# Spreading the last 128 tokens of an attention-then-experts kernel over four wider chunks

## The chip, the core and the metric

The kernel runs on one core of a Trainium2 chip. The metric is the device time of one execution, in microseconds (us), on that core; lower is better.

## The reference

A polynomial-sketch attention feeds a mixture of four dense experts. All inputs and outputs are float32.

```python
# attention: batch 4, heads 4, sequence 1088, head_dim 32, r = 8
phi = lambda x: outer(S1 @ x, S2 @ x)              # 64 features a token
num, den = phi(q) @ (phi(k).T @ v), phi(q) @ phi(k).sum(0)
x = (num / (den + 1e-6)).reshape(4352, 128)        # tokens x (heads*head_dim)
# experts: D = 128, E = 4, F = 1024
p = domain_probs / (domain_probs.sum(-1, keepdims=True) + 1e-9)
for e in range(4):
    out += p[:, e:e+1] * (np.maximum(x @ w1[e], 0) @ w2[e])
```

Nearly all arithmetic is in the experts: every token passes four times through a 128x1024 and a 1024x128 matrix.

## The kernel before

**Chunks.** The 4352 tokens are worked off in 11 chunks (`CHUNKS`, L101): chunk 0 of 128 tokens, chunk 1 of 448, chunks 2 and 3 of 480, chunks 4 to 9 of 448, chunk 10 of 128. Each chunk has 16 steps (`NQ`), four for each expert; a step handles two blocks of 128 hidden units. A half step is one block, and the program numbers half steps from the start: 32 to a chunk, so half step 160 is the first of chunk 5. The order of all work is written out by hand in half steps: which part of the attention runs when (`FIRST_AT`, `KEYS_AT`, `UNITS_AT`, L824 to L834), and which matmul of the second layer runs how many half steps after its expert began (`DEAL`, `DEAL_MORE`, `DEAL_ALL`, L75 to L88).

**A wide chunk** (1 to 9) computes with split operands: a float32 operand is replaced by two or three parts that TensorE multiplies at the fast float32 rate. The first layer of a block is three matmuls into one PSUM buffer: L1171, L1172, then a copy in place on ScalarE (L1173), then L1223. The second layer of a block is either three split matmuls (L1295 with `ha`, `hb`, `hd`), for which ScalarE makes `ha` (L1227), VectorE `hb` (L1199) and, for two blocks at once, `hd` (L1202); or one *plain* float32 matmul (L1295 with `hid`), for which ScalarE alone makes `hid` (L1232). Which blocks are split is fixed for each chunk and expert: six (`THREE`), seven (`MORE_IN`) or eight (`ALL_IN`).

**Closing an expert.** The second layer adds up in two PSUM banks, `o0` and `o1`. ScalarE copies `o0` to `ev` (L1298; one buffer); in the last chunks it copies `o1` to `rest` (L1331) and GpSimd adds `rest` to `ev` (L1334; in earlier chunks VectorE adds `o1`, L1328). GpSimd then multiplies by the gate (L1341) and adds to the chunk's running `total` (L1343), each in two pieces. After the fourth expert VectorE transposes `total` (L1306) and SyncE stores it with four DMAs (L1309).

**Narrow chunks** (0 and 10) are computed plainly: `both` (L274) splits each matmul in halves of 64 columns (all on L272), for chunk 10 the first three steps use L1141; ReLU is on ScalarE (L1149) and VectorE (L1145) in turn; the gate is applied by VectorE (L1260, L1264), and one DMA stores the result (L1269). The first-layer and second-layer weights in float32 have been overwritten by their parts by then, so `load_last` (L988) reads them again in the middle of chunk 9. Chunk 10's tokens are the last 128 of batch 3, so the loads of batch 3's queries, of the gate's probabilities and the stores treat that batch's rows in two pieces (L128, L326, L566, L1313).

**Attention beside it.** For the last three batches, a *unit* of 512 or 576 query tokens is projected, stored to a scratch tensor and read back in two arrangements (`unit_rows`, L797 and L799, four transfers of 256 or 288 KB on SyncE's queue), multiplied on VectorE (`unit_product`, L811, two halves) and then attended (`unit_visit`). Each row of `UNITS_AT` gives, for a unit, the half steps of its transpose, of its two products and of its visit; a unit's `unit_rows` follows the visit of the unit before. So for unit 5 the transfers are issued at half step 175, and its products stand at 191 and 196.

Of the kernel before, what the change touches and what calls it, by code (L numbers as in the profile page):

```python
# [24 lines left out]
def kernel(  # L25
# [24 lines left out]
    nc = tc.nc  # L50
# [17 lines left out]
    FULL = 3  # L68
# [19 lines left out]
    )  # L88
    ALL_IN = {(7, 2), (8, 2), (9, 2)}
# [11 lines left out]
    CHUNKS = [P, 448, 480, 480] + [448] * 6 + [P]  # L101
    NC = len(CHUNKS)
    MORE_IN = {(2, 2), (3, 2), (4, 2), (5, 0), (5, 2), (5, 3), (6, 2), (7, 0), (7, 1), (7, 2), (7, 3), (8, 0), (8, 1), (8, 2), (8, 3), (9, 0), (9, 1), (9, 2), (9, 3)}
    MORE_AT = {0: (61, 62), 1: (56, 57), 2: (38, 39), 3: (77, 78)}
# [16 lines left out]
    def load_rows(src, b, name, part=slice(0, S)):  # L121

        d = kn if name == "kn" else qn
        if b not in d:
            d[b] = lpool.tile([P, S], F32, tag=name, name=name)
        c, n = part.start, part.stop - part.start
        base = src.offset + b * H * S * D
        if name == "qn" and b == B - 1:  # L128
            for c, n, t in ((0, (G - 4) * D, 0), ((G - 4) * D, 4 * D, S - P)):
                nc.sync.dma_start(d[b][:, c : c + n], bass.AP(src.tensor, base + t * D, [[S * D, H], [n, 32], [1, n]]))  # L130
        else:
            nc.sync.dma_start(d[b][:, part], bass.AP(src.tensor, base + c, [[G * D, P], [1, n]]))
# [34 lines left out]
    def load_w2(e, k, to=None):  # L167
        of = OTHER if k else THREE
        w2_of[e, k] = cpool.tile([P, len(of) * DM], F32, tag=f"w2_{e}{k}", name="w2_sb")[:, :] if to is None else to
        runs = []  # L170
        for b in of:
            if runs and b == runs[-1][1]:
                runs[-1][1] += 1
            else:
                runs.append([b, b + 1])
        for b, z in runs:
            at = split_at(b)
            nc.sync.dma_start(
                w2_of[e, k][:, DM * at : DM * (at + z - b)].rearrange("p (g d) -> p g d", d=DM),
                w2[e, P * b : P * z].rearrange("(g p) d -> p g d", p=P),  # L180
            )
# [7 lines left out]
    def three_of(m, e):  # L189
        return tuple(range(FB)) if (m, e) in ALL_IN else MORE if more(m, e) else THREE  # L190

    def deal_of(m, e):
        return DEAL_ALL if (m, e) in ALL_IN else DEAL_MORE if more(m, e) else DEAL
# [24 lines left out]
    ends = cpool.tile([P, 2, E], F32, name="ends")  # L218
    e_sum = cpool.tile([P, 2, 3], F32, name="e_sum")
# [106 lines left out]
    for p0, n, g0, m, t in ((0, 96, 0, G, 0), (96, 32, 0, G - 4, 3 * S), (96, 32, G - 4, 4, B * S - P)):  # L326
        nc.scalar.dma_start(
            _ap(dp, p0, n, g0 * E, [[1, m * E]]),
            bass.AP(domain_probs.tensor, domain_probs.offset + t * E, [[m * E, n], [1, m * E]]),
        )  # L330
    for i, t, g in ((0, 0, G), (1, B * S - P, 4)):
        nc.gpsimd.dma_start(
            ends[:, i, :], bass.AP(domain_probs.tensor, domain_probs.offset + t * E, [[g * E, 32], [1, 4 * E]])
        )
# [11 lines left out]
    def gate_sums():  # L346
        add = lambda out, in0, in1: nc.gpsimd.tensor_tensor(out=out, in0=in0, in1=in1, op=ALU.add)
        nc.gpsimd.memset(pn[:, G * E :], 0.0)
        add(e_sum[:, :, 0:2], ends[:, :, 0:2], ends[:, :, 2:4])
        add(e_sum[:, :, 2], e_sum[:, :, 0], e_sum[:, :, 1])  # L350
# [4 lines left out]
    def gate_quotients():  # L355
        nc.vector.tensor_scalar(
            out=e_sum[:, :, 2], in0=e_sum[:, :, 2], scalar1=1e-9, scalar2=1.0, op0=ALU.add, op1=ALU.mult
        )
        nc.vector.reciprocal(e_sum[:, :, 2], e_sum[:, :, 2])
        for i in range(2):  # L360
            nc.vector.tensor_scalar(
                out=ends[:, i, :], in0=ends[:, i, :], scalar1=e_sum[:, i, 2:3], scalar2=None, op0=ALU.mult
            )
# [37 lines left out]
    x_last = cpool.tile([P, P], F32, name="x_last")  # L401
    ring = cpool.tile([P, 3 * CW], F32, name="ring")
    PLACES = [(0, P, x_first, 0), (P, START[3], ring, 3 * CW - START[3] + P)]
    PLACES += [(START[m], START[m + 1], ring, (m - 3) % 3 * CW) for m in range(3, NC - 1)]
    PLACES += [(START[-1], B * S, x_last, 0)]
# [158 lines left out]
    def unit_parts(b, c, n):  # L564

        return [(0, n - P), (n - P, P)] if b == B - 1 and c + n == S else [(0, n)]  # L566

# [4 lines left out]
    def query_turns(b, c, n, qT):  # L572


        for c0, m in unit_parts(b, c, n):
            src = c + c0
            if b == c == 0:
                todo = [([[1, m]], [[1, m]], 0, 0)]
            elif c0:
                todo = [([[32, 4], [1, 32]], [[1, 4], [4, 32]], 0, 0)]  # L580
            else:
                T = blocks(m)
                if T[0] == T[1]:
                    todo = [([[32 * T[0], 4], [32, T[0]], [1, 32]], [[32, 4], [P, T[0]], [1, 32]], 0, 0)]
                else:
                    todo = [
                        ([[32 * T[s], 2], [32, T[s]], [1, 32]], [[32, 2], [P, T[s]], [1, 32]], 64 * T[0] * s, HP * s)
                        for s in range(2)
                    ]
            for i, o, ci, co in todo:  # L590
                nc.vector.transpose(_ap(qT, 0, P, c0 + co, o), _ap(qn[b], 0, P, src + ci, i))
                yield
# [66 lines left out]
    def attend_products(b, c, n, qp):  # L659

        nd = [psum(ps_h, "h") for _ in range(1 if sum(blocks(m)[0] for _, m in unit_parts(b, c, n)) < 4 else 2)]
# [3 lines left out]
        for c0, m in unit_parts(b, c, n):  # L665
# [154 lines left out]
    def add(hs, run):  # L820
# [12 lines left out]
        (172, 191, 196, 207), (200, 217, 219, 223),  # L833
# [152 lines left out]
    w_last = {}  # L986

    def load_last():  # L988

        for e, (tag, width) in enumerate((("kn", S), ("vn", H * NT * D), ("qn", S), ("vx", NT * H * (D + 1)))):  # L990
            w1_of[e] = (cpool if tag == "vx" else lpool).tile([P, width], F32, tag=tag, name="w1_last")
            nc.sync.dma_start(w1_of[e][:, 0:F], w1[e])
            if e == 0:
                w_last[0] = apool.tile([P, E - 1, N3 * DM], F32, tag="kp", name="w2_last")
                w_last[1] = cpool.tile([P, N3 * DM], F32, tag="kT", name="w2_last")
            load_w2(e, 0, w_last[0][:, e] if e < E - 1 else w_last[1][:, :])

# [101 lines left out]
    def plain(m):  # L1099
        return m in (0, NC - 1)  # L1100
# [21 lines left out]
    def first(i, work, between=None):  # L1122
# [3 lines left out]
        if plain(m):  # L1126
# [7 lines left out]
            elif i in made_hp:  # L1134
                hp = made_hp.pop(i)
            else:
                hp = psum(ps_h, "h")
                for j in range(2):
                    w = w1_of[e][:, P * (2 * f + j) : P * (2 * f + j + 1)]
                    if m and kq < FULL:  # L1140
                        nc.tensor.matmul(hp[:, n * j : n * j + n], w, x_last[:, :], start=True, stop=True)  # L1141
                    else:
                        both(hp[:, n * j : n * j + n], w, (x_last if m else x_first)[:, :], start=True, stop=True)
            if m and kq % 2:
                nc.vector.tensor_scalar(  # L1145
                    out=hd[:, 0 : 2 * n], in0=hp[:, 0 : 2 * n], scalar1=0.0, scalar2=None, op0=ALU.max
                )
            else:
                nc.scalar.activation(hd[:, 0 : 2 * n], hp[:, 0 : 2 * n], ACTF.Relu)  # L1149
# [17 lines left out]
        for j in range(2):  # L1167
            k = 2 * f + j
            g = psum(ps_h, "h")[:, 0:n]
            w = slice(P * k, P * (k + 1))  # L1170
# [63 lines left out]
    def second(i, j=None):  # L1234
# [4 lines left out]
        if plain(m):  # L1239
# [16 lines left out]
            if f == NP - 1:  # L1256
                p_e = ends[:, 1 if m else 0, e : e + 1]
# [9 lines left out]
                if e == E - 1:  # L1267
                    t, to = (B * S - P, [[DM, P], [1, DM]]) if m else (0, [[G * DM, 32], [1, 4 * DM]])
                    nc.sync.dma_start(bass.AP(out.tensor, out.offset + t * DM, to), total.pop(m)[:, :])  # L1269
# [14 lines left out]
    def passed(m, e, what, k, hd):  # L1284
# [9 lines left out]
        w, h = (second_weight(e, k), hd) if what == "x" else (w2_parts[e][k]["abd".index(what)], hd["abd".index(what)])  # L1294
        nc.tensor.matmul(acc[m, e][o][:, 0:n], w, h, start=first_one, stop=last)  # L1295
        if last and o == 0:
            evs[m, e] = mpool.tile([P, CW], F32, tag="ev", bufs=1, name="ev")
            nc.scalar.activation(evs[m, e][:, 0:n], acc[m, e][0][:, 0:n], ACTF.Copy, scale=1.0 + R12)  # L1298
        if last and o == 1:
            close(m, e)  # L1300

    def turn_back(m, src):
# [4 lines left out]
        for b, c, nn, at in parts(m):  # L1307
            for a in range(4):
# [4 lines left out]
                        [[(G - 4 if b == B - 1 else G) * DM, 32], [DM, nn // 32], [1, 32]],  # L1313
# [4 lines left out]
    def gather(m, e):  # L1318
# [27 lines left out]
        if not plain(later):  # L1346
            load_gates(later, [(e + 2) % E])
        if e == E - 1:
            yield
            yield  # L1350

            for _ in range(0 if m + 2 < NC else 4):
                yield
# [28 lines left out]
    for m in range(2, NC - 1):  # L1382
# [53 lines left out]
    for i in range(len(steps) + LA):  # L1436
        if i < len(steps):
# [13 lines left out]
            if kq == NQ - 4 and 0 < m < NC - 2:  # L1451
# [20 lines left out]
            if m == NC - 2 and kq == NQ // 2:  # L1472
                assert have[0] == B * S and not plan
                load_last()
# [5 lines left out]
        if NQ * (NC - 1) <= i < NQ * (NC - 1) + 2:  # L1480
            continue
        if not behind(2 * i + 1):
            next(ending, None)

# [28 lines left out]
```

## Time and profile before

| | |
|---|---|
| median of 3 runs | 445.8 us (445.8 to 446.19) |
| the profiled execution | 445.93 us |
| its span, first to last instruction | 444.1 us |
| TensorE busy | 438.3 us (99%) |
| VectorE / ScalarE / GpSimd busy | 382.7 / 341.9 / 166.5 us |
| TensorE's granted clock | 1.00 of full |

The span is 1.8 us shorter than the time: what lies around the instructions. "Busy" is the union of an engine's instruction times; TensorE's matmuls overlap, and a busy TensorE is one that always has a matmul in flight. In a timeline a row gives start, duration, engine, line, operation, what it writes and reads, and in brackets the idle time before it with what ended it. The pace of TensorE is read from the starts of successive matmuls, not from their durations.

### The profile page before, as it was taken

The numbers are of one execution on the slowest core, as the hardware profiler recorded it, in microseconds if no ns is written. First come the engines' busy times: TensorE is split into PE (matmuls) and PEld (weight loads), VectorE is DVE, ScalarE is ACT, GpSimd is POOL, SyncE is SP. The second block draws the span as 40 slices with busy tenths as digits, with TensorE's granted clock in tenths as the row PEclk, the third lists the DMA queues.
The fourth block names the chain that finished last, engine by engine and source line by source line (L and its number), as shares of the span: only waits on it lengthen the run. The fifth ranks groups of instructions, "written<-read, shape, count | busy, mean of one in ns | idle before, by whom it ended". The sixth has DMA issues, their size and how long they took to land.

```text
span 444.1 us, 8644 instructions
## 1 busy us (share of the span) xinstructions
PE 438.3 (99%) x2995; PEld 371.3 (84%) x2995; DVE 382.7 (86%) x624; ACT 341.9 (77%) x731; POOL 166.5 (37%) x249
## 2 busy tenths in 40 slices
PE   8999999999999999999999999999999999999996
PEld 5887678888887888888888888888889888888986
DVE  5998969978999889989997998799989898998942
ACT  4478888858877688868885888687888888988831
POOL 7348523312142023313341353133445634554560
PEclk9999999999999999999999999999999999999999
DMA  6966375224502340245024601352201120015601
GB/s 175 288 183 166 84 171 118 77 50 122 156 24 45 106 107 22 63 91 142 22 43 88 124 21 32 89 126 53 57 21 21 25 61 22 21 42 173 202 1 29
DMA packets 51156, 38.46 MB, mean 87 GB/s; under 512 B 24968, under 2 KB 45384, under 8 KB 51112
## 3 DMA queue, kind: packets, MB, share of 16 engines
q1 hardware_dynamic: 49672, 36.79, 32.8%
q0 software_dynamic: 1216, 1.06, 1.1%
q8 instruction: 23, 0.38, 0.4%
q14 instruction: 21, 0.17, 0.1%
q10 hardware_dynamic: 224, 0.07, 0.1%
HBM read 32.68 MB, written 5.21 MB: 85 GB/s over the span
## 4 chain that ended last, share of the span: by engine, by line
PE 94%; DMA 4%; DVE 1%; issue 0%; ACT 0%; POOL 0%; SPq 0%; DVEq 0%; ACTq 0%
PE o L1295 40%; PE h L1223 13%; PE h L1171 13%; PE h L1172 13%; PE h L272 7%; PE o L1277 3%; PE o L272 3%; DMA w_sb<-in_moe_w_dram 3%; PE h L467 1%; DMA dp<-in_moe_domain_probs_dram 1%; DVE hb L1199 0%; DMA s_raw<-in_S_dram 0%; PE h L1141 0%; DVE qp L811 0%; DVE words L281 0%
## 5 line engine op out<-in xcount | busy, mean ns | idle before, releaser
L1173 ACT ACTIVATE h<-h 128x448 f32<-128x448 f32 (+1 forms) x288 | 155.5, 540 | 60.3 <-PE h L1172 54.6
L1199 DVE SCALAR_TENSOR_TENSOR hb<-h,ha 128x448 fp32r<-128x448 f32 (+1 forms) x226 | 137.0, 621 | 24.5 <-ACT ha L1227 22.5
L1202 DVE SCALAR_TENSOR_TENSOR hd<-ha,hb 128x896 fp32r<-128x896 f32 (+3 forms) x121 | 135.0, 1116 | 12.4 <-PE o L1295 1.1
L1171 PE MATMUL h<-xa,wa 128*128 128x448 f32 (+1 forms) x288 | 127.0, 441 | 0.0
L1227 ACT ACTIVATE ha<-h 128x448 fp32r<-128x448 f32 (+1 forms) x226 | 124.1, 549 | 0.0
L1223 PE MATMUL h<-xd,wd 128*128 128x448 f32 (+1 forms) x288 | 106.9, 371 | 0.1
L1172 PE MATMUL h<-xb,wb 128*128 128x448 f32 (+1 forms) x288 | 106.2, 369 | 0.0
L1341 POOL TENSOR_TENSOR ev<-ev,gate 128x256 f32<-128x256 f32 (+2 forms) x54 | 46.2, 855 | 139.1 <-DVE ev L1328 131.5
L1295 PE MATMUL o<-ha,vab 128*128 128x448 f32 (+1 forms) x204 | 75.8, 371 | 0.0
L1171 PEld LDWEIGHTS h<-xa,wa 128*128 128x128 f32 x288 | 54.2, 188 | 15.7 <-issue 10.7
L1172 PEld LDWEIGHTS h<-xb,wb 128*128 128x128 f32 x288 | 54.2, 188 | 15.5 <-issue 11.1
L1295 PE MATMUL o<-hd,vd 128*128 128x448 f32 (+1 forms) x204 | 62.4, 373 | 0.0
L1223 PEld LDWEIGHTS h<-xd,wd 128*128 128x128 f32 x288 | 54.0, 187 | 7.6 <-ACT h L1173 1.4
L1343 POOL TENSOR_TENSOR total<-total,ev 128x256 f32<-128x256 f32 (+2 forms) x54 | 55.9, 1035 | 4.2
L1295 PE MATMUL o<-hb,vb 128*128 128x448 f32 (+1 forms) x136 | 50.3, 370 | 0.4 <-DVE hb L1199 0.4
L1334 POOL TENSOR_TENSOR ev<-ev,rest 128x256 f32<-128x256 f32 (+1 forms) x28 | 19.9, 731 | 69.8 <-ACT rest L1331 69.8
L1295 PE MATMUL o<-hid,w_sb 128*128 128x448 f32 (+1 forms) x92 | 43.0, 549 | 0.0
L1295 PEld LDWEIGHTS o<-hd,vd 128*128 128x128 f32 x204 | 37.8, 188 | 4.7 <-issue 0.8
L1295 PEld LDWEIGHTS o<-ha,vab 128*128 128x128 f32 x204 | 38.3, 188 | 3.8
L1232 ACT ACTIVATE hid<-h 128x448 f32<-128x448 f32 (+1 forms) x62 | 34.2, 551 | 1.0 <-PE h L1223 0.8
L1295 PEld LDWEIGHTS o<-hb,vb 128*128 128x128 f32 x136 | 25.5, 188 | 3.6 <-DVE hb L1199 1.1
L1341 POOL TENSOR_TENSOR total<-ev,gate 128x256 f32<-128x256 f32 (+2 forms) x18 | 14.9, 848 | 35.3 <-issue 19.9
(159 smaller groups left out, 500.2 us busy)
## 6 DMA issues: line engine op xcount, KB each, us to landing
gate<-gates SPq DMA_DIRECT2D x22, 224.0 KB, 3.3
kn<-in_k_dram SPq DMA_DIRECT2D x4, 544.0 KB, 6.9
vn<-in_v_dram SPq DMA_DIRECT2D x16, 128.0 KB, 4.6
qp<-qd SPq DMA_DIRECT2D x8, 256.0 KB, 3.3
w_last<-in_moe_w_dram SPq DMA_DIRECT2D x4, 512.0 KB, 5.6
qp<-qd SPq DMA_DIRECT2D x6, 288.0 KB, 4.9
qb<-qd SPq DMA_DIRECT2D x6, 288.0 KB
w_sb<-in_moe_w_dram SPq DMA_DIRECT2D x3, 512.0 KB
```

The costliest lines, as they stand in the source:

```text
L272: nc.tensor.matmul(out(s), weights(s), moving(s), **flags)
L1171: nc.tensor.matmul(g, wa[:, e, w], xa, start=True, stop=False)
L1172: nc.tensor.matmul(g, wb[:, e, w], xb, start=False, stop=True)
L1173: nc.scalar.activation(g, g, ACTF.Copy, scale=1.0 + R12)
L1199: nc.vector.scalar_tensor_tensor(out=hb, in0=g, scalar=0.0, in1=high, op0=ALU.max, op1=ALU.subtract)
L1202: nc.vector.scalar_tensor_tensor(out=d2, in0=a2.bitcast(F32), scalar=R12, in1=b2.bitcast(F32), op0=ALU.mult, op1=ALU.subtract)
L1223: nc.tensor.matmul(g, w, x, start=False, stop=True, skip_group_check=True)
L1227: nc.scalar.activation(ha, g, ACTF.Relu, scale=NEAR)
L1232: nc.scalar.activation(hid[i][j], g, ACTF.Relu)
L1295: nc.tensor.matmul(acc[m, e][o][:, 0:n], w, h, start=first_one, stop=last)
L1341: nc.gpsimd.tensor_tensor(out=to[:, x], in0=ev[:, x], in1=g[:, x], op=ALU.mult)
L1343: nc.gpsimd.tensor_tensor(out=total[m][:, x], in0=total[m][:, x], in1=ev[:, x], op=ALU.add)
```

## The change

The last chunk goes; its 128 tokens are given to chunks 4 to 7, which become 480 tokens wide. The order is now 128, 448, six chunks of 480, two of 448. What goes with it: `load_last`, the two-piece treatment of batch 3 and of the probabilities. The last expert of the last chunk (9, 3) splits six blocks instead of seven, in the order `THREE + OTHER`, so that the two plain blocks come last (`DEAL_END`); the last plain matmul is made in two halves of 224 tokens; GpSimd applies the gate to `o0` alone, VectorE to `o1`, adds, transposes and stores each half by itself (`finish`), with the DMAs alternating between SyncE's and ScalarE's queues. Two places in the hand-written order move: a split of expert 0's weights (`MORE_AT`) from steps 61, 62 to 73, 75, and unit 5's first product from half step 191 to 180.

```diff
+    DEAL_END = dict(
+        a0=4, b0=4, a1=4, b1=5, a2=5, a3=5, d0=6, d1=6, b2=6, a4=7, b3=7, a5=8, b4=8, d2=8, d3=8,
+        b5=9, d4=10, d5=10, x6=10, x7=11,
+    )
...
-    CHUNKS = [P, 448, 480, 480] + [448] * 6 + [P]
+    CHUNKS = [P, 448] + [480] * 6 + [448] * 2
...
-    MORE_AT = {0: (61, 62), 1: (56, 57), 2: (38, 39), 3: (77, 78)}
+    MORE_AT = {0: (73, 75), 1: (56, 57), 2: (38, 39), 3: (77, 78)}
...
-        (172, 191, 196, 207), (200, 217, 219, 223),
+        (172, 180, 196, 207), (200, 217, 219, 223),
...
-    for p0, n, g0, m, t in ((0, 96, 0, G, 0), (96, 32, 0, G - 4, 3 * S), (96, 32, G - 4, 4, B * S - P)):
-        nc.scalar.dma_start(
...
+    nc.scalar.dma_start(
+        _ap(dp, 0, P, 0, [[1, G * E]]), bass.AP(domain_probs.tensor, domain_probs.offset, [[G * E, P], [1, G * E]])
+    )
...
-    def load_last():
...
     def plain(m):
-        return m in (0, NC - 1)
+        return m == 0
+    def at_end(m, e):
+        return (m, e) == (NC - 1, E - 1)
...
+        for x in halves(n) if last and o and at_end(m, e) else [slice(0, n)]:
+            nc.tensor.matmul(acc[m, e][o][:, x], w, h[:, x], start=first_one, stop=last, skip_group_check=at_end(m, e))
         if last and o == 0:
             evs[m, e] = mpool.tile([P, CW], F32, tag="ev", bufs=1, name="ev")
             nc.scalar.activation(evs[m, e][:, 0:n], acc[m, e][0][:, 0:n], ACTF.Copy, scale=1.0 + R12)
+            if at_end(m, e):
+                ev, g = evs.pop((m, e)), gate[m, e]
+                for x in halves(n):
+                    nc.gpsimd.tensor_tensor(out=ev[:, x], in0=ev[:, x], in1=g[:, x], op=ALU.mult)
+                    nc.gpsimd.tensor_tensor(out=total[m][:, x], in0=total[m][:, x], in1=ev[:, x], op=ALU.add)
         if last and o == 1:
-            close(m, e)
+            finish(m, e) if at_end(m, e) else close(m, e)
+    def finish(m, e):
+        n = CHUNKS[m]
...
+        for x in halves(n):
+            nc.vector.tensor_tensor(out=rest[:, x], in0=g[:, x], in1=o1[:, x], op=ALU.mult)
+            nc.vector.tensor_tensor(out=rest[:, x], in0=rest[:, x], in1=whole_sum[:, x], op=ALU.add)
+            nc.vector.transpose(ob[:, x], rest[:, x])
+            t, r = (c + x.start) // 32, (x.stop - x.start) // 32
+            for a in range(4):
+                (nc.scalar if a % 2 else nc.sync).dma_start(
...
```

## The prediction

> **What bounds the kernel.** I read the page's busy shares first, then the chain that ended last, then the busy time by chunk, then TensorE's rows, and last what runs after the last wide matmul.
>
> ```profile
> PE 438.3 (99%) x2995; PEld 371.3 (84%) x2995; DVE 382.7 (86%) x624; ACT 341.9 (77%) x731; POOL 166.5 (37%) x249
> ...
> PE 94%; DMA 4%; DVE 1%; issue 0%; ACT 0%; POOL 0%; SPq 0%; DVEq 0%; ACTq 0%
> ```
>
> TensorE is 94% of the chain, so a matmul added in the middle is time added, and one removed is time saved, unless TensorE waits there. By chunk (4 to 8, and the end from TensorE's first narrow matmul on):
>
> ```profile
> core 0: us, PE busy (x) PEld busy (x) DVE busy (x) ACT busy (x) POOL busy (x), PEclk, DMA share, GB/s
> 173.34:216.09 42.75, 42.75 (x234) 35.98 (x233) 39.42 (x59) 33.97 (x73) 12.45 (x15) 1.00 0.33 82
> 216.09:259.98 43.89, 43.89 (x299) 38.44 (x298) 38.56 (x60) 34.32 (x73) 14.49 (x17) 1.00 0.35 70
> 259.98:304.56 44.58, 44.21 (x267) 37.21 (x266) 39.96 (x64) 33.70 (x71) 14.70 (x17) 1.00 0.28 67
> 304.56:343.90 39.34, 39.34 (x189) 35.24 (x188) 35.46 (x53) 34.72 (x75) 15.14 (x17) 1.00 0.21 43
> 343.90:383.47 39.57, 39.57 (x191) 35.42 (x189) 35.54 (x49) 34.91 (x74) 19.39 (x23) 1.00 0.14 30
> ...
> 423.10:444.10 21.00, 17.45 (x258) 16.27 (x257) 7.56 (x16) 5.01 (x12) 6.61 (x9) 1.00 0.09 16
> ```
>
> First number: length of the stretch. TensorE fills the chunks that grow (only the third has 0.37 us of idle), and VectorE, at 39.42 of 42.75, is not far behind it. The change buys the narrow chunk's time with wider matmuls in four chunks, so the forecast is a difference of two numbers near 10 us.
>
> **1. Four chunks grow by 32 tokens.** Chunks 4 to 7 hold 171, 177, 171 and 183 split matmuls, 702 in all, and 7, 5, 7 and 3 plain ones, 22. The pace is read from starts in the chain: two pieces of chunk 2 (480 tokens) and two of chunk 8 (448), in each case six matmuls apart.
>
> ```profile
> 110.29 0.65 PE o L1295 x3
> 111.60 0.65 PE o L1295 x3
> ...
> 351.13 0.61 PE o L1295 x3
> 352.35 0.61 PE o L1295 x3
> ```
>
> (111.60 - 110.29)/6 = 0.218 us against (352.35 - 351.13)/6 = 0.203; two decimals allow a difference of 0.0143 to 0.0150, and I take 0.0147: 702 x 0.0147 = 10.3 us. A piece with a plain matmul (one split, then two passes) takes 1.02 us at 480 and 0.95 at 448 in the same chain, so a plain one grows by 0.07 - 0.015 = 0.055: 22 x 0.055 = 1.2 us. **Sum +11.5.** From above 702 x 0.0150 + 1.2 = 11.7; from below, by the durations of L1223 (379 against 369 ns), 702 x 0.010 + 1.2 = 8.2, which is far off because durations overlap. Check: 183 x 0.203 + 3 x 0.75 = 39.4 for chunk 8, measured 39.57. ScalarE and VectorE grow less (L1199 from 614 to 646 ns, 5%) and stay behind TensorE's 7%.
>
> The Trainium skill ("TensorE: Matmul & The Clock Gate", Back-to-back issue gap) says that successive warm matmuls start N/2.4 + 2.5 ns apart; as an estimate 32 columns would then cost 13.3 ns, not 14.7, and the four passes of a plain one 53 ns: 10.5 us in place of 11.5.
>
> **2. The end.** TensorE's order is the same in both kernels up to the last matmul of expert (9, 2), at 418.69 us before. What follows lasts 444.1 - 418.7 = 25.4 us before, narrow chunk included.
>
> ```profile
> 418.69 0.36 PE L1295 MATMUL o<-hd,vm 128*128 128x448 f32 x1
> ...
> 425.39 0.60 POOL L1343 TENSOR_TENSOR total<-total,ev 128x192 f32<-128x192 f32 x1
> 426.46 0.55 ACT L1298 ACTIVATE ev<-o 128x448 f32<-128x448 f32 x1 [1.10 <-PE o L1295]
> ...
> 430.51 0.73 POOL L1343 TENSOR_TENSOR total<-total,ev 128x256 f32<-128x256 f32 x1
> 431.20 0.60 POOL L1341 TENSOR_TENSOR ev<-ev,gate 128x192 f32<-128x192 f32 x1
> ...
> 440.61 0.35 DVE L1264 SCALAR_TENSOR_TENSOR end<-o,ends,end 128x128 f32<-128x128 f32 x1 [0.89 <-PE o L272]
> 440.99 0.36 SPq L1269 DMA_DIRECT2D out_dram<-end  x1
> ```
>
> After, in the times of before: TensorE still has 28 split matmuls (5.7 us) and two plain blocks (0.75 each) from 418.89 on, so it is done at about 426.2. GpSimd is later. It closes expert (9, 2) at 425.99 (second row: 425.39 + 0.60), and `ev` has one buffer, so ScalarE can't copy `o0` of (9, 3) earlier: 426.04 to 426.6 (L1298, 0.55). Behind that copy on ScalarE stand only its four store DMAs. Then four GpSimd operations of 224 columns, 0.67 each (between 0.60 for 192 and 0.73 for 256), with 0.06 between: the first half of `total` at 428.1, the second at 429.45. VectorE has made the first product of gate and `o1` by 426.4 and waits: add (0.38, between L1328's 0.61 for 448 and L477's 0.415 for 256), transpose (0.37 by L1306), second product, done at 429.3; its second add waits for GpSimd.
>
> That first add reads two SBUF operands while GpSimd works. Before, L1343 takes 1.61 us for 256 columns beside L1202, which reads two, and 0.73 alone. So I add 0.3: second half of `total` at 429.75. [...]
>
> Second add to 430.2, transpose to 430.6, two stores per queue of about 0.5 to issue, the last issued at 431.1. Before, from the issue of the last store (440.99) to the end of the span is 3.15 us; stores of 128-byte rows (L1309) land 1.5 to 1.9 us after issue, the last one before (512-byte rows) 1.6, so I keep 3.15. **End at 434.3, 9.8 us earlier**; 9.1 if GpSimd is blocked by the transposes too (0.3 each), 10.3 without any block and with faster landings.
>
> **3. Unit 5's first product moves from half step 191 to 180.** At 191 it costs TensorE this wait, because an `hb` stands behind it on VectorE; the matmul before started at 262.84, 0.74 us earlier instead of 0.20, so about 0.55 us goes away:
>
> ```profile
> 263.58 0.47 PE L1295 MATMUL o<-hb,vb 128*128 128x448 f32 x1 [0.37 <-DVE hb L1199]
> ```
>
> At 180 it stands between the two `hb` of these rows:
>
> ```profile
> 245.97 0.61 DVE L1328 TENSOR_TENSOR ev<-ev,o 128x448 f32<-128x448 f32 x1
> 246.50 1.15 DVE L1199 SCALAR_TENSOR_TENSOR hb<-h,ha 128x448 fp32r<-128x448 f32 x2
> ```
>
> VectorE would get there at 247.1, or 247.6 with the wider columns. Its operand `qb` was issued on SyncE's queue at 243.12, as the second of four transfers of 288 KB. L797's transfers land 3.3 to 6.1 us after issue: 246.4 to 249.2. The DMA share in these microseconds is 0.5 to 0.95, so I take the late end, 249.2. Then the product (0.75 to 1.15, both seen in L811) ends at 250.0 to 250.4, and the `hb`, `hd`, `hb` behind it at 250.6, 251.9 and 252.5. TensorE takes these at 249.9, 251.1 and 250.9 before, about 0.8 later after; the last is late by 0.5 to 1.0. I take **+0.75 for the new wait, -0.55 for the old one**; bounds 0 and 2.0 for the new.
>
> **4. The start.** The probabilities take one DMA instead of three, so the weight loads behind them, which are issued only as earlier DMAs land, come sooner. TensorE waits for a weight once, 0.33 us at 20.48: **-0.3**, bounds -0.33 and 0. The repeated weight loads of chunk 9 (0.40 DMA share there) hid behind TensorE: 0. The split moved by `MORE_AT` only changes chunk: 0. With narrower gate arithmetic, likewise.
>
> **Sum:** 11.5 - 9.8 - 0.55 + 0.75 - 0.3 = +1.6 on 445.93 us, the profiled time; this is 0.13 above the median, so **447.4 us**, slightly slower.
>
> **Rivals.** (a) *Cheaper columns*: if 32 more cost what the durations of L1295's `hb` rows grow by (367 to 380 ns), the four chunks grow by 702 x 0.013 + 1.2 = 10.3, and the time is 446.2. For it: L1172 grows by 15, L1223 by 10; against: the starts above, which are what TensorE's time is made of. The rule of the Trainium skill's page on TensorE falls here too (10.5). (b) *The transfer is there in time*, since the earliest landing is 246.4: no new wait, 0.75 less, 446.65. Decided by whether `qb` lands before 247.6. (c) *The wait is long*: VectorE has little slack in chunk 5 (38.56 of 43.89 busy), and GpSimd's work at 247 to 250 stretches its operations (L1202 1.48 us instead of 1.09 there); 2 us and more, 449. (d) *Faster*: VectorE is the real bound in chunks 4 to 7. Then these grow only by its growth: 106 `hb` by 32 ns and 53 `hd` by 48 ns (1172 to 1220), with some 0.6 for the rest 6.5 us in place of 11.5, and the time is 442.4. For it: 92% busy in chunk 4 and the wait at 263.58. Against: it holds only if TensorE waits for VectorE by over some 2.6 us in these chunks, and it is idle for 0.37.
>
> **Chances.** Forecast 0.50, (a) 0.10, (b) 0.15, (c) 0.12, (d) with other unseen savings 0.13. Faster or slower by over 0.2% means past 444.9 or 446.7, about what a measurement of this kernel tells from no change. (a) and (b) are within that, the forecast and (c) above it: slower 0.62, same 0.25, faster 0.13. The range leaves out (d) and the worst of (c): 445.4 to 449.0. The bounds of the steps (growth up to 11.7, end 9.1 to 10.3, wait 0 to 2.0) lie in it.
>
> **What would show it.** Chunks 4 to 7 together 11 to 12 us longer, with L1295 triplets 0.65 apart; a wait of VectorE before L811's counterpart near half step 180 and TensorE waiting for an `hb` after it, and none at chunk 6's start; from the last matmul of (9, 2) to the end about 15.6 us, the last add waiting for GpSimd, not for TensorE. I am wrong if the four chunks grow by under 10 us, if the tail is under 14.5 us, or if new waits of TensorE on VectorE appear in chunk 4, where it is busiest.

## The result, and the profile after

The changed kernel takes **448.22 us** (median; 448.15 to 448.93) against 445.87 for the kernel before on the same chip: ratio 1.0055, 95% interval 1.0042 to 1.0068. It is 0.55% slower. In what follows *before* and *after* are short for the two kernels. The profiled execution of after took 448.93 us with a span of 446.86, and so lies 0.7 above the median; its start, the latest of nine (experiment 7), would account for that.

The page of the kernel after, busy shares and the chain that ended last:

```profile
PE 435.2 (97%) x2752; PEld 357.7 (80%) x2752; DVE 385.4 (86%) x612; ACT 345.9 (77%) x722; POOL 168.3 (38%) x246
...
PE 89%; DMA 4%; POOL 2%; DVE 1%; SPq 1%; ACT 1%; issue 1%; POOLq 0%; DVEq 0%; ACTq 0%
```

TensorE has 3.1 us less to do and leads 89% of the chain instead of 94%: GpSimd has come in with 2%, at the end. The same chunks as before (4 to 8), from the first wide matmul of one chunk to that of the next:

```profile
core 0: us, PE busy (x) PEld busy (x) DVE busy (x) ACT busy (x) POOL busy (x), PEclk, DMA share, GB/s
173.93:219.19 45.26, 45.26 (x234) 36.17 (x233) 40.73 (x60) 36.16 (x75) 12.17 (x15) 1.00 0.29 79
219.19:267.33 48.14, 47.22 (x299) 38.17 (x298) 41.05 (x61) 36.24 (x73) 14.66 (x17) 1.00 0.33 66
267.33:314.11 46.78, 46.78 (x268) 37.44 (x266) 40.97 (x63) 35.41 (x71) 15.73 (x17) 1.00 0.25 65
314.11:356.16 42.05, 42.05 (x189) 35.23 (x188) 37.49 (x52) 36.65 (x75) 16.16 (x17) 1.00 0.21 42
356.16:395.92 39.76, 39.76 (x191) 35.41 (x190) 35.65 (x49) 34.97 (x74) 20.44 (x23) 1.00 0.14 31
```

Chunks 4 to 7 are 2.51, 4.25, 2.20 and 2.71 us longer, 11.67 together; chunk 8, no wider, 0.19. The odd ones are the second (TensorE idle for 0.92) and the third (before, it held 0.37 of idle; now none). From chunk 9's start to the end it takes 446.86 - 395.92 = 50.94 us, against 444.14 - 383.47 = 60.67 before. The rest is in the start: TensorE's first matmul of chunk 1 stands at 29.08 instead of 28.57.

The idle of chunk 5, in the timeline of VectorE, of TensorE and of SyncE's queue (rows as in the prediction):

```profile
251.43 0.65 DVE L1168 SCALAR_TENSOR_TENSOR hb<-h,ha 128x480 fp32r<-128x480 f32 x1
254.06 1.07 DVE L793 TENSOR_TENSOR qp<-qp,qb 128x576 f32<-128x576 f32 x1 [1.99 <-DMA qb<-qd]
255.06 0.64 DVE L1168 SCALAR_TENSOR_TENSOR hb<-h,ha 128x480 fp32r<-128x480 f32 x1
```

```profile
254.88 0.37 PE L1265 MATMUL o<-ha,vab 128*128 128x480 f32 x1
255.76 0.49 PE L1265 MATMUL o<-hb,vb 128*128 128x480 f32 x1 [0.51 <-DVE hb L1168]
...
256.74 0.37 PE L1265 MATMUL o<-ha,vab 128*128 128x480 f32 x1
257.52 0.49 PE L1265 MATMUL o<-hb,vb 128*128 128x480 f32 x1 [0.41 <-DVE hb L1168]
```

```profile
248.05 0.62 SPq L781 DMA_DIRECT2D qb<-qd  x1
```

VectorE stands at unit 5's first product (L793, the L811 of before) for 1.99 us, until `qb`, issued at 248.05, is there, 6.0 us after its issue. Two `hb` behind it come late. Starts of successive matmuls are 0.22 apart here; 255.76 - 254.88 = 0.88 and 257.52 - 256.74 = 0.78 are 0.66 and 0.56 too long, and the matmul behind each is another 0.10 to 0.11 late: some 1.45 us lost.

The end, in the timeline:

```profile
437.15 1.67 PE L1265 MATMUL o<-hid,w_sb 128*128 128x448 f32 x6
...
437.81 0.59 POOL L1339 TENSOR_TENSOR total<-total,ev 128x192 f32<-128x192 f32 x1
...
438.43 0.54 ACT L1268 ACTIVATE ev<-o 128x448 f32<-128x448 f32 x1 [1.31 <-POOL total L1339]
...
439.79 0.66 POOL L1273 TENSOR_TENSOR total<-total,ev 128x224 f32<-128x224 f32 x1
440.40 0.66 POOL L1272 TENSOR_TENSOR ev<-ev,gate 128x224 f32<-128x224 f32 x1
440.48 0.83 DVE L1289 TENSOR_TENSOR rest<-rest,total 128x224 f32<-128x224 f32 x1 [1.18 <-POOL total L1273]
441.14 0.68 POOL L1273 TENSOR_TENSOR total<-total,ev 128x224 f32<-128x224 f32 x1
...
442.13 0.39 DVE L1289 TENSOR_TENSOR rest<-rest,total 128x224 f32<-128x224 f32 x1
```

TensorE is done at 438.8. VectorE's first product of gate and `o1` still waits for it, but then stands 1.18 us until GpSimd has the first half of `total` (the brackets of the row at 440.48). So the end hangs on GpSimd's closing of (9, 2) (L1339, done at 438.40), ScalarE's copy into the one `ev` buffer, and GpSimd's operations, as forecast. The last row has no wait in brackets: the second add did not wait for GpSimd.

### The profile page after: what moved, and what is told of

Same layout as the page of the kernel before. It is cut to its first block, busy times and chain, and to the rows that moved or that the text cites. A ratio compares the mean times of both kernels' runs of the same rounds, so it can differ in the third digit from the quotient of the medians.

```text
span 446.9 us, 8094 instructions
## 1 busy us (share of the span) xinstructions
PE 435.2 (97%) x2752; PEld 357.7 (80%) x2752; DVE 385.4 (86%) x612; ACT 345.9 (77%) x722; POOL 168.3 (38%) x246
## 4 chain that ended last, share of the span: by engine, by line
PE 89%; DMA 4%; POOL 2%; DVE 1%; SPq 1%; ACT 1%; issue 1%; POOLq 0%; DVEq 0%; ACTq 0%
PE o L1265 39%; PE h L1140 13%; PE h L1141 13%; PE h L1192 13%; PE h L271 6%; PE o L1245 3%; DMA w_sb<-in_moe_w_dram 2%; PE h L458 1%; DMA qb<-qd 1%; PE o L271 1%; DMA dp<-in_moe_domain_probs_dram 1%; SPq L177 1%; POOL total L1339 0%; ACT h L1142 0%; DMA s_raw<-in_S_dram 0%
## 5 line engine op out<-in xcount | busy, mean ns | idle before, releaser
L1142 ACT ACTIVATE h<-h 128x480 f32<-128x480 f32 (+1 forms) x288 | 158.8, 552 | 63.4 <-PE h L1141 58.3
L1168 DVE SCALAR_TENSOR_TENSOR hb<-h,ha 128x480 fp32r<-128x480 f32 (+1 forms) x225 | 140.6, 639 | 27.6 <-ACT ha L1196 25.8
L1171 DVE SCALAR_TENSOR_TENSOR hd<-ha,hb 128x960 fp32r<-128x960 f32 (+3 forms) x120 | 137.8, 1149 | 11.7 <-DVE hb L1168 0.5
L1140 PE MATMUL h<-xa,wa 128*128 128x480 f32 (+1 forms) x288 | 129.4, 449 | 0.0
L1196 ACT ACTIVATE ha<-h 128x480 fp32r<-128x480 f32 (+1 forms) x225 | 126.2, 561 | 1.7 <-PE h L1192 1.6
L1192 PE MATMUL h<-xd,wd 128*128 128x480 f32 (+1 forms) x288 | 108.7, 377 | 0.1
L1141 PE MATMUL h<-xb,wb 128*128 128x480 f32 (+1 forms) x288 | 108.0, 375 | 0.0
L1265 PE MATMUL o<-ha,vab 128*128 128x480 f32 (+1 forms) x204 | 76.8, 377 | 0.0
L1140 PEld LDWEIGHTS h<-xa,wa 128*128 128x128 f32 x288 | 54.2, 188 | 17.8 <-issue 11.3
L1265 PE MATMUL o<-hd,vd 128*128 128x480 f32 (+1 forms) x204 | 63.7, 379 | 0.0
L1339 POOL TENSOR_TENSOR total<-total,ev 128x256 f32<-128x256 f32 (+2 forms) x52 | 55.1, 1060 | 4.1
L1265 PE MATMUL o<-hb,vb 128*128 128x480 f32 (+1 forms) x136 | 51.4, 378 | 0.9 <-DVE hb L1168 0.9
```

Source lines behind the costliest of these rows:

```text
L1140: nc.tensor.matmul(g, wa[:, e, w], xa, start=True, stop=False)
L1141: nc.tensor.matmul(g, wb[:, e, w], xb, start=False, stop=True)
L1142: nc.scalar.activation(g, g, ACTF.Copy, scale=1.0 + R12)
L1168: nc.vector.scalar_tensor_tensor(out=hb, in0=g, scalar=0.0, in1=high, op0=ALU.max, op1=ALU.subtract)
L1171: nc.vector.scalar_tensor_tensor(out=d2, in0=a2.bitcast(F32), scalar=R12, in1=b2.bitcast(F32), op0=ALU.mult, op1=ALU.subtract)
L1192: nc.tensor.matmul(g, w, x, start=False, stop=True, skip_group_check=True)
```

## The experiments

**1. The new wait.** Two kernels change one number each, the half step of unit 5's first product (191 in the one, 183 in the other).

```diff
-        (172, 180, 196, 207), (200, 217, 219, 223),
+        (172, 191, 196, 207), (200, 217, 219, 223),
+        (172, 183, 196, 207), (200, 217, 219, 223),
```

Expected of the product back at 191, its place before:

> Unit 5's first product goes back to half step 191, as before; all else as in the changed kernel (448.2). Theory, late transfer: the 1.45 us that TensorE loses around 255 to 257 us comes only from VectorE waiting 2.0 us for the second transfer of unit 5; it goes, and the wait at the start of chunk 6 comes back with at most 0.55, less with 480 columns: 447.0 to 447.4, and no wait of VectorE for that transfer. Rival, loaded VectorE: chunk 5 is too full for the product wherever it stands, and a wait of the same size appears at 191: 448.0 or more.

Expected at 183:

> Unit 5's first product at half step 183 instead of 180, some 4 us later; all else as in the changed kernel (448.2). Theory, late transfer: VectorE gets there at about 256, after the transfer has landed (254), and the product of 0.75 to 1.1 us fits into the 1.9 to 2.6 us by which the operands there are ahead of TensorE: no wait, 446.7 to 446.9. Rival, loaded VectorE: 448.0.

At 191 it took 447.35 us (ratio to before 1.0027, 1.0018 to 1.0036), at 183 446.67 (1.0015, 1.0006 to 1.0024). Chunk 5 goes from 48.14 to 46.69 and 46.70 long. At 191 the old wait is back in chunk 6, 47.31 long; at 183 that chunk keeps 46.78. The rival, a VectorE too loaded for the product wherever it stands, gave 448.0 or more for both and is out. In the timeline of the kernel at 183 the product no longer waits, and takes 0.75:

```profile
254.50 1.16 DVE L1171 SCALAR_TENSOR_TENSOR hd<-ha,hb 128x960 fp32r<-128x960 f32 x1
255.57 0.75 DVE L793 TENSOR_TENSOR qp<-qp,qb 128x576 f32<-128x576 f32 x1
```

So the new wait costs 1.45 and the old one 0.53, and neither is needed. 446.67 is also what rival (b) of the prediction, the transfer in time, had given for half step 180 (446.65); as it came out, that describes the product at 183.

**2. The old wait alone,** in the kernel before.

```diff
-        (172, 191, 196, 207), (200, 217, 219, 223),
+        (172, 186, 196, 207), (200, 217, 219, 223),
```

> The kernel before with unit 5's first product at half step 186 instead of 191, all else as before. Theory: at 191 it delays an hb that TensorE waits for, and the transfer (landed by 249.2) is there at 186: chunk 6 starts without the wait of 0.37 us and chunk 5 with 6 together are 0.55 us shorter, 445.3 us. Rival: the slack is shared, and the product takes VectorE's time wherever it stands, so the wait only moves: 445.9.

445.24 us against 445.90 (ratio 0.9982, 0.9974 to 0.9991). Chunk 6 went from 44.58 to 43.94, all others kept their length: the wait was worth 0.64, and it went rather than moved.

**3. What the wider columns cost.** The kernel before with its product at 186 (first fence, chunks 4 to 7 of 448 tokens) and the changed kernel with its product at 183 (second fence, 480) both keep TensorE busy throughout these chunks, so their lengths give the growth alone:

```profile
173.42:216.17 42.75, 42.75 (x234) 35.98 (x233) 39.44 (x59) 33.99 (x73) 12.46 (x15) 1.00 0.32 82
216.17:260.08 43.91, 43.91 (x299) 38.44 (x298) 38.77 (x61) 34.33 (x73) 14.48 (x17) 1.00 0.34 70
260.08:304.02 43.94, 43.94 (x267) 37.31 (x266) 39.22 (x63) 33.52 (x71) 14.96 (x17) 1.00 0.26 68
304.02:343.38 39.36, 39.36 (x189) 35.26 (x188) 35.50 (x53) 34.76 (x75) 15.17 (x17) 1.00 0.20 43
```

```profile
173.05:218.31 45.26, 45.26 (x234) 36.15 (x233) 40.75 (x60) 36.17 (x75) 12.19 (x15) 1.00 0.29 79
218.31:265.01 46.70, 46.70 (x299) 38.43 (x298) 41.39 (x62) 36.21 (x73) 15.62 (x17) 1.00 0.34 68
265.01:311.79 46.78, 46.78 (x267) 37.43 (x266) 40.92 (x63) 35.37 (x71) 15.58 (x17) 1.00 0.24 65
311.79:353.87 42.08, 42.08 (x189) 35.23 (x188) 37.48 (x52) 36.64 (x75) 16.15 (x17) 1.00 0.21 42
```

180.82 - 169.96 = 10.86 us, and 0.17 more in chunk 8, where the second layer of chunk 7's last blocks still runs: 11.0.

**4. One part alone: no narrow chunk and the new ending, without the wider chunks.**

```diff
-    CHUNKS = [P, 448] + [480] * 6 + [448] * 2
+    CHUNKS = [P, 448] + [480] * 2 + [448] * 6
...
-        (172, 180, 196, 207), (200, 217, 219, 223),
+        (172, 191, 196, 207), (200, 217, 219, 223),
```

> One part of the change alone: the narrow chunk is gone and the new ending is in, but chunks 4 to 7 stay 448 wide and unit 5's first product stays at half step 191; the last 128 tokens are left uncomputed. Theory (growth 11.5 us by the starts of matmuls, end 9.8): 445.87 - 9.8 - 0.3 = 435.8 us, lengths of chunks 4 to 7 as in the kernel before (42.8, 43.9, 44.6, 39.3), and the kernel with the product back at 191 (447.35) is 11.5 us above it. Rival (a) (columns cost what the durations show, and part of after's growth is something else): the difference is 10.3 to 10.5. Rival (d) (VectorE is the bound, growth 6.5): the difference is under 8.

437.19 us (ratio 0.9803, 0.9789 to 0.9816), 1.4 more than expected, and 10.2 below the kernel with the product at 191, where 11.5 was expected and rival (a) gave 10.3 to 10.5. That doesn't speak for (a), because this kernel has waits that the other hasn't. The end is as in after (50.90); chunk 4 is 43.25 long instead of 42.75, and chunk 5 44.31 instead of 43.89. In chunk 4 stands a wait that neither before nor after has. Its timeline, VectorE and then TensorE:

```profile
203.01 0.83 DVE L898 SCALAR_TENSOR_TENSOR vm<-w_sb,vm 128x128 fp32r<-128x128 f32 x1
203.76 0.61 DVE L1170 SCALAR_TENSOR_TENSOR hb<-h,ha 128x448 fp32r<-128x448 f32 x1
204.41 1.51 DVE L1173 SCALAR_TENSOR_TENSOR hd<-ha,hb 128x896 fp32r<-128x896 f32 x1
```

```profile
205.76 0.37 PE L1267 MATMUL o<-ha,vab 128*128 128x448 f32 x1
206.51 0.47 PE L1267 MATMUL o<-hb,vb 128*128 128x448 f32 x1 [0.38 <-DVE hb L1170]
```

L898 is the split of expert 0's seventh block, which the change moves into chunk 4 (`MORE_AT`). Another kernel puts it back into chunk 3:

```diff
-    MORE_AT = {0: (73, 75), 1: (56, 57), 2: (38, 39), 3: (77, 78)}
+    MORE_AT = {0: (61, 62), 1: (56, 57), 2: (38, 39), 3: (77, 78)}
```

> The kernel with 448 columns throughout and the last 128 tokens left uncomputed, with the split of expert 0's seventh block back at steps 61, 62 as in the kernel before. Theory: the split in chunk 4 (VectorE's 0.83 us between two hb) is what cost TensorE the wait of 0.54 + 0.11 us in chunk 4, which is free only where the chunk is 480 wide: 437.19 - 0.65 = 436.5, chunk 4 42.75 long as before; the wait of 0.24 at the unit's product in chunk 5 stays or goes with it (436.3). Rival: the wait in chunk 4 comes from the earlier start of the kernel (transfers land later against the work), and stays: 437.2.

436.41 us (0.9788, 0.9775 to 0.9801), and chunk 4 is 42.75 again: the moved split was the cause. Chunk 5 keeps 0.3 more than in the kernel before (44.20 against 43.89), which was not followed. In after the moved split costs nothing that shows: TensorE has no idle in chunk 4. The likely reason is that a chunk of 480 leaves VectorE more slack (4.5 of 45.26 us in chunk 4, against 3.3 of 42.75). The kernel with all tokens and the product at 191 is 447.35 - 436.41 = 10.9 us above this one. That is a rougher measure of the growth than the lengths of the chunks: this kernel waits 0.3 us more in chunk 5 and some 0.2 more in chunk 6 (44.63 against 43.94 without a wait; the other has 47.31 against 46.78), and starts differ by tenths.

**5. What ends the kernel.** First the new ending is undone: (9, 3) closes like the experts before it.

```diff
-            if at_end(m, e):
-                ev, g = evs.pop((m, e)), gate[m, e]
...
-            finish(m, e) if at_end(m, e) else close(m, e)
+            close(m, e)
```

> After without the new ending of the last expert's result: order of blocks and chunks as after, but (9, 3) is closed as the other experts of chunk 9 are (ScalarE copies o1, GpSimd adds it, gates and adds to total, then one transpose and four stores). Theory (GpSimd ends the work): behind GpSimd's closing of (9, 2) at 438.4 stand, after ScalarE's two copies, six GpSimd operations (two of each kind, 0.6 and 0.73 us with 0.06 between, 4.2 us) where after has four of 0.66 of which only the last is waited for, then a transpose of 448 columns (0.75) and four stores on one queue: from chunk 9's start to the end 2 to 3 us more than after's 50.94, 450.2 to 451.2 us. Rival: TensorE's last matmul at 438.8 and the stores set the end, and the halves only overlap what is hidden: under 1 us more, 448.5 to 449.2.

450.36 us (ratio to before 1.0097, 1.0084 to 1.0111), 2.1 above after, and 53.42 from chunk 9's start to the end. Its timeline shows GpSimd ending it, with one transpose and four stores behind:

```profile
438.67 1.27 POOL L1325 TENSOR_TENSOR ev<-ev,rest 128x256 f32<-128x256 f32 x2 [1.20 <-ACT rest L1322]
439.90 0.72 POOL L1332 TENSOR_TENSOR ev<-ev,gate 128x256 f32<-128x256 f32 x1
...
442.05 0.59 POOL L1334 TENSOR_TENSOR total<-total,ev 128x192 f32<-128x192 f32 x1
442.67 0.65 DVE L1297 STREAM_TRANSPOSE ob<-total 128x448 f32<-128x448 f32 x1 [7.01 <-POOL total L1334]
```

Second, GpSimd's load ahead of the ending is made lighter: VectorE adds `o1` to `ev` in the closing of (9, 2), as in earlier chunks.

```diff
-            if m < 7 and (m, e) not in FAR_ADD:
+            if (m < 7 and (m, e) not in FAR_ADD) or (m, e) == (NC - 1, E - 2):
```

> When the last expert but one of the last chunk closes, VectorE adds o1 to ev in one operation, in place of ScalarE's copy and GpSimd's two additions; all else as in the changed kernel (448.2). Theory, GpSimd bounds the end: its closing of that expert starts and ends some 2 us sooner, ScalarE's copy of o0 no longer waits for it, and the end is bound by TensorE's last matmul and VectorE's six operations: 1.2 to 1.5 us less, 446.7 to 447.0. Rival, TensorE or the stores bound the end: no change, 448.2, or up to 0.5 more where VectorE's extra operation makes TensorE wait.

446.75 us (1.0019, 1.0008 to 1.0030); from chunk 9's start to the end 49.78, 1.16 less. Now TensorE's last matmul comes last, in its timeline:

```profile
436.57 1.67 PE L1265 MATMUL o<-hid,w_sb 128*128 128x448 f32 x6
...
438.28 0.39 DVE L1288 TENSOR_TENSOR rest<-gate,o 128x224 f32<-128x224 f32 x1 [2.28 <-PE o L1265]
...
438.77 0.59 DVE L1289 TENSOR_TENSOR rest<-rest,total 128x224 f32<-128x224 f32 x1
```

The product of the first half starts at 438.28, though that half's last matmul record ends at 437.87; the second half's ends at 438.24. It looks as if it waits for both, so that the two halves of the matmul buy nothing.

**6. The versions that follow.** Both mendings together (product at 183, VectorE's add):

> After with both mendings at once: unit 5's first product at half step 183, and VectorE instead of ScalarE and GpSimd adding o1 to ev in the closing of expert (9, 2). If the new wait and GpSimd's closing are two separate costs (one in chunk 5, the other behind chunk 9), they add: 446.67 - 1.16 = 445.5 us, chunk 5 46.7 us long and 49.8 us from chunk 9's start to the end; beside 445.87 of the kernel before the ratio is 0.999. Rival: the kernel with VectorE's add gained by a luckier start and not by its end, so that only part adds: 446.2.

445.35 us (0.9987, 0.9979 to 0.9996), chunk 5 46.70, end 49.79: they add up. Then the last matmul and its product in one piece of 448 columns:

```diff
-        for x in halves(n) if last and o and at_end(m, e) else [slice(0, n)]:
-            nc.tensor.matmul(acc[m, e][o][:, x], w, h[:, x], start=first_one, stop=last, skip_group_check=at_end(m, e))
+        nc.tensor.matmul(acc[m, e][o][:, 0:n], w, h[:, 0:n], start=first_one, stop=last)
...
+        nc.vector.tensor_tensor(out=rest[:, 0:n], in0=g[:, 0:n], in1=o1[:, 0:n], op=ALU.mult)
         for x in halves(n):
-            nc.vector.tensor_tensor(out=rest[:, x], in0=g[:, x], in1=o1[:, x], op=ALU.mult)
```

> Both mendings (unit 5's first product at half step 183, VectorE's add in the closing of (9, 2)), and now the last plain matmul in one piece of 448 columns instead of two halves, and one product of gate and o1 of 448 columns instead of two; adds, transposes and stores stay in halves. Theory: the halves of the matmul buy nothing, since the first product started at 438.28 in the kernel with VectorE's add, 0.04 behind the end of the second half's last record and 0.41 behind the first half's; one product (0.61 for 448 columns) in place of 0.39 and 0.35 ends VectorE's chain 0.1 to 0.2 earlier, and the stores with it: 49.6 from chunk 9's start to the end instead of 49.79, time 445.2. Rival: the first half's stores are what the end waits for (four on two queues before the second half's four), and they start 0.2 later: 50.0, time 445.55.

445.04 us (0.9984, 0.9976 to 0.9993), end 49.63: the theory's number, though the times of these two kernels overlap. In its timeline the second add follows 0.04 us behind GpSimd's last addition (437.49 + 0.71, add at 438.24), so GpSimd's queue sets the end again, if only by a tenth: VectorE's transpose before that add ends at 438.13. Both kernels are faster than the kernel before, and neither can be told from that kernel with its own product moved (445.24). What gained over the kernel before was the waits that went; that moving the tokens gains anything by itself isn't shown.

**7. The start.** The probabilities again in three DMAs, with the same data.

```diff
-    nc.scalar.dma_start(
-        _ap(dp, 0, P, 0, [[1, G * E]]), bass.AP(domain_probs.tensor, domain_probs.offset, [[G * E, P], [1, G * E]])
-    )
+    for p0, n, g0, m in ((0, 96, 0, G), (96, 32, 0, G - 4), (96, 32, G - 4, 4)):
+        nc.scalar.dma_start(
...
```

> The probabilities come in three DMAs on ScalarE's queue again (96x136, 32x120 and 32x16), in the plain layout; all else as in the changed kernel (448.2), whose first wide matmul starts 0.5 us later than before's. Theory, issue order: with one DMA instead of three more weight loads are in flight sooner and the one that TensorE waits for (expert 2's first layer, landing at 20.8 instead of 20.3) takes 7.4 us instead of 5.7; three DMAs put that back: first wide matmul at 28.6, time 447.7. Rival, chance: transfers scatter by some tenths from run to run, and neither the start nor the time moves with the number of DMAs: 448.2.

448.28 us (1.0049, 1.0033 to 1.0065), as after; in its profile chunk 1 starts at 28.45. The other profiles give: 28.57 and 28.57 with the start of before; with one DMA 29.08 in after and 28.01 to 28.50 in eight others (mean 28.19). So the start scatters by some tenths, and after's profile is the worst of nine. By these means one DMA gains 0.3 to 0.4, by the medians (448.22 against 448.28) nothing: it can't be told from the scatter.

## Why the prediction was right

The time was 0.8 us above the forecast and within its range, and the sign held. By the steps:

| step | forecast | measured | by |
|---|---|---|---|
| chunks 4 to 7 grow | +11.5 | +11.0 | 10.86 + 0.17, both kernels without waits |
| the end | -9.8 | -9.73 | 60.67 to 50.94 |
| old wait | -0.55 | -0.64 | kernel before, product at 186 |
| new wait | +0.75 | +1.45 | 48.14 to 46.70 in chunk 5 |
| start | -0.3 | -0.4, unsure | mean of eight profiles; +0.5 in after's own |
| sum | +1.6 | +1.7 | |

That the two sums agree to 0.1 is luck: the growth was 0.5 too large and the new wait 0.7 too small. The medians differ by 2.35. Of the 0.65 left, some 0.3 lies outside the span: the time minus the span is 2.07 us in the profiled run of after and 1.79 in that of before, and it lies anywhere between 1.8 and 2.2 in the profiled runs of the other kernels. The rest, 0.35, was not placed; the row of the start is unsure by as much.

**The growth** was right in kind, 0.5 too large: the mechanism is TensorE's start-to-start time. The prediction's reading of its four starts was too narrow: they are rounded to 0.01 us, which leaves the difference between 0.0117 and 0.0183 us, not 0.0143 to 0.0150, and so didn't exclude rival (a)'s 0.013. Over the successive split matmuls (more than 900 pairs each, in the kernel before with its product at 186 and in after with its product at 183) the time from start to start is 203.3 ns at 448 and 217.7 at 480, 14.4 apart instead of 14.7, and a plain matmul's pass grows from 376 to 403, so 702 x 0.0144 + 22 x 0.054 = 11.3. The last 0.3, down to the 11.0 of the chunks' lengths, was not followed. Rival (a) is too low, by the pace (13 ns against 14.4) and by the lengths (10.3 against 11.0), though the lengths lie only 0.5 below the forecast and 0.7 above (a); rival (d), 6.5, is out. The Trainium skill ("TensorE: Matmul & The Clock Gate", Back-to-back issue gap) gives N/2.4 + 2.5 ns as the gap of an isolated warm matmul, 189.2 and 202.5 for these widths; the trace disagrees with 203.3 and 217.7, and the page's slope, 13.3 per 32 columns, is 1.1 short.

**The end** came out to 0.1 by luck, as two errors cancelled. The step that failed is the block: GpSimd was to lose 0.3 to VectorE's first add. GpSimd's operations kept 0.66 to 0.68; it was the add that took 0.83 instead of 0.39. It started at 440.48, 0.08 behind GpSimd's L1272, and ended 0.24 after that one ended. So VectorE's own chain, and not GpSimd, set the last add. The row from which the forecast took the block had the other order; there VectorE started 0.07 ahead of GpSimd:

```profile
423.08 1.09 DVE L1202 SCALAR_TENSOR_TENSOR hd<-ha,hb 128x896 fp32r<-128x896 f32 x1
423.15 1.61 POOL L1343 TENSOR_TENSOR total<-total,ev 128x256 f32<-128x256 f32 x1
```

The trace of after bears the order out. Of GpSimd's closing operations of 224 columns, the 13 that started ahead of an overlapping `hd`, product or last add of VectorE kept 0.66 to 0.68 us; the 15 that started behind one took 1.60 in the median. The Trainium skill ("SBUF — State Buffer", Who interferes with whom) says that issue order decides who is blocked; the rows agree, though the rest of the add after GpSimd's end, 0.24, is shorter than a whole add.

**The new wait** is the term that was mis-sized, 0.75 for 1.45. The transfer came 6.0 us after its issue, near the late end of 6.1 that the prediction took, and the product took 1.07, near its upper bound, where it took 0.75 at 183: in after, GpSimd's L1339 was running as it started (253.85 to 254.52). That much of rival (c) was so, and the 1.45 lies about halfway between the forecast's 0.75 and (c)'s 2 us. What failed is "about 0.8 later after": the time at which TensorE wants the `hb`. From chunk 5's start to the issue it is 27.03 us before and 28.86 after (+1.83), to TensorE's demand of the first `hb` 33.8 and 35.9 (+2.1). Wider columns move both, so the demand is later by only 0.3 against the transfer. The prediction had set a shifted demand beside an unshifted issue. With 0.3 in place of 0.8 not only the last `hb` but already the first comes late, and the two waits of the timeline follow.

**The old wait** went as forecast. `MORE_AT` at nothing was right for after; with chunks of 448 it costs 0.5 us in chunk 4 and 0.8 in the time (437.19 against 436.41).

## What to carry to other kernels

When columns are added to a matmul-bound stretch, price them by the distance of starts over a whole chunk, and shift every time in it, the issues of transfers included, before a new wait is sized. A removed tail and wider chunks cancelled here to 1.3 us; two waits and one engine's queue at the end were worth as much, and each was mended in one line. Before you let one engine hold up another in a forecast, look which of the two starts first. An operation that has moved at no cost may be hidden by slack: undo what made the slack, and it shows.

## What was not expected of the hardware

- An add of 224 columns on VectorE with both operands in SBUF takes 0.39 us with GpSimd at rest (after's second add, at 442.13). Started 0.08 us behind an operation of GpSimd (after) it took 0.83, and 0.31 behind one (VectorE's add) 0.59; both ended 0.24 after GpSimd's operation. Started 0.54 behind one (one product) it kept 0.39, and ended 0.27 after it. That the one holds the other up is read from these rows and from the order above; no run took GpSimd's operation away at this place.
